# Two-kind attention and a four-expert MoE on one core: softmax sums by ones beside the values, exp(-ln) on ScalarE, an fp32 first group, and loads in another order

## The chip, the cores and the metric

The kernel runs on one core of a Trainium2 chip. A core has five engines, each with a queue of its own that it works through in order: TensorE (PE in the profile; its weight loads are PEld), VectorE (DVE), ScalarE (ACT), GpSimd (POOL) and SyncE (SP). DMAs are issued from SP, ACT and POOL; POOL's are the ones that can convert fp32 to fp16 on the way. The metric is the device time of one execution in microseconds, lower is better. Each time here is the median of three runs.

## The reference

Attention over 4 batches, 8 heads, 768 positions, head size 64, followed by a dense mixture of four experts. Heads 0, 2 and 6 are retrieval heads (plain causal); the five others are streaming heads, which see the first 4 positions and a window of 64.

```python
scores = scale * np.matmul(q, k.transpose(0, 1, 3, 2))
stream_keep = causal & (is_sink | in_win)          # n_sink = 4, window = 64
scores = np.where(mask, scores, -1e9); scores -= scores.max(-1, keepdims=True)
a = np.exp(scores); a = a / (a.sum(-1, keepdims=True) + 1e-9)
attn = np.matmul(a, v)                             # (4, 8, 768, 64)
x = attn.transpose(0, 2, 1, 3).reshape(3072, 512)
p = domain_probs / (domain_probs.sum(-1, keepdims=True) + 1e-9)
for e in range(4):
    out += p[:, e:e+1] * (np.maximum(x @ w1[e], 0) @ w2[e])   # 512 -> 1024 -> 512
```

The kernel takes exp without subtracting the maximum; the inputs are small.

## The kernel before

**Groups.** The 3072 rows are cut into eight groups of 384 rows, two per batch (`c` = 0 and 1). For each group there is an attention part, `attention(b, c)`, that leaves the transposed attention output `xT[g]` (512 x 384, fp16), and a MoE part, `moe_group(g)`, that needs it. The first half of a batch has scores against up to 384 keys, the second against up to 768 in retrieval heads.

**MoE.** Per expert, layer 1 is eight banks of four matmuls of 384 columns (L489), each bank evicted by a Relu on ScalarE (L496) into `hs`; layer 2 is three output tiles of eight matmuls of 512 columns (L502), each tile scaled by the row's probability and added into `acc` on VectorE (L514, L518). The weights of all experts stay in SBUF as fp16.

**Attention.** q and k arrive as fp16 and are transposed on PE against an identity (L302), two heads at a time (`transposes(hp)`); q goes to `qT` through ScalarE (L310), k to `kz` through VectorE (L317, L321, L326). `kz` is zero where the other head of the pair lies; in streaming heads it is kept in tiles of 96 keys with the 4 sink keys in front. `scores(h)` multiplies (L372), takes exp on ScalarE (L381) into `es` and multiplies by a 0/1 mask on VectorE (L385). `values(h)` multiplies `es` by v, with a column of ones as 65th column, so that row 64 of the PSUM bank holds the sums (L412). The sums go to `srow` (L425) and by a small DMA on SP into row h of `sums32` (L428); the values go to `av32` (L431). When all eight heads are through, three reciprocals (L461) and a cast (L463) make `rec16`, four matmuls with a selection matrix `sel` spread it over the partitions (L468), and four multiplies give `xT` (L475).

**Order.** Every engine's order is the order of the code. Attention of group 0 stands alone ahead of everything. After that the attention of group g + 1 is a generator whose steps are put between the steps of `moe_group(g)`, at a rate set by `begin`, `end` and `ATT`. All steps of the attention, the selection matmuls too, are thus spread over the MoE part before.

**Memory.** PSUM has eight banks: five for `pA` (transposes, scores, layer 1, the spread of the sums), one `pV`, two `pO`.

**Start.** k of group 0 comes as fp32 by SP and is cast on VectorE (L189), v as fp32 by ScalarE's and SP's queues and is cast between the heads (L196, L200, with the sink rows in L203), q by POOL with conversion (L178). POOL then builds the masks, loads w1 and w2 of expert 0, q, k and v of group 1, and the other weights, one DMA per head for q, k and v (L132, L133, L144). The kernel uses eight semaphores in turn for POOL's DMAs, so that the ninth waits until the first has landed.

Of the kernel before, what the change touches and what calls it, by code (L numbers as in the profile page):

```python
# [16 lines left out]
def kernel(  # L17
# [59 lines left out]
    )  # L77


    def bank():  # L80
        return pA.tile([P, 512], FP32, name="pA", bufs=5)
# [7 lines left out]
    vSf = []  # L89
    DV = D + 2  # L90
    for i in range(2):
        kz.append(
            [
                pers.tile([P, NT, P] if not RETR[h] else [P, S], FP16, name=f"kz{i}_{h}")
                for h in range(H)
            ]
        )
        vR.append(pers.tile([P, S // P, len(RH), DV], FP16, name=f"vR{i}"))
        vSf.append(pers.tile([P, NT * len(SH) * DV], FP16, name=f"vS{i}"))
        vS.append(vSf[i].rearrange("p (t s d) -> p t s d", t=NT, s=len(SH)))  # L100
# [12 lines left out]
    p_sb = pers.tile([P, NTILE, E], FP32, name="p_sb")  # L113

# [14 lines left out]
    def load_qk(b, c):  # L129
        alloc_qk(b, c)  # L130
        for h in range(H):
            nc.gpsimd.dma_start(out=q16[b, c][:, :, h, :], in_=rows_of(q, b, h, c))  # L132
            nc.gpsimd.dma_start(out=k16[b, c][:, :, h, :], in_=rows_of(k, b, h, c))  # L133
# [12 lines left out]
    def sink_rows(b):
        i = b % 2
        nc.vector.tensor_copy(
            out=vS[i][0:NS, :, :, 0:D],
            in_=vS[i][R0 : R0 + NS, 0:1, :, 0:D].to_broadcast([NS, NT, len(SH), D]),  # L150
        )

    def load_w1(e, f0, f1):
        nc.gpsimd.dma_start(
# [4 lines left out]
    def load_w2(e):  # L159
        nc.gpsimd.dma_start(  # L160
            out=w2sb[:, e * FTP : (e + 1) * FTP, :],
            in_=moe_w2[e].rearrange("(fo fi) d -> fi fo d", fi=P),
        )
# [4 lines left out]
    v32 = moe.tile([P, 4, H, D], FP32, name="v32", tag="hs", bufs=2)

    def load_v32(eng, h):  # L170
        if RETR[h]:
            eng.dma_start(out=v32[:, 0:3, h, :], in_=rows_of(v, 0, h, 0))
        else:
            eng.dma_start(out=v32[R0:P, :, h, :], in_=tiles_of(v, 0, h, 0))

    make_identity(nc, ident16)
    for h in range(H):
        nc.gpsimd.dma_start(out=q16[0, 0][:, :, h, :], in_=rows_of(q, 0, h, 0))  # L178
        nc.sync.dma_start(out=k32[:, :, h, :], in_=rows_of(k, 0, h, 0))
        if h < H // 2:  # L180
            load_v32(nc.scalar, h)
    for h in range(H // 2, H):
        load_v32(nc.sync, h)
    nc.sync.dma_start(
        out=probs, in_=moe_domain_probs.rearrange("(t p) e -> p t e", p=P)
    )

    def cast_k(hp):
        nc.vector.tensor_copy(  # L189
            out=k16[0, 0][:, :, 2 * hp : 2 * hp + 2, :],  # L190
            in_=k32[:, :, 2 * hp : 2 * hp + 2, :],
        )

    def cast_v(h):
        if RETR[h]:
            nc.vector.tensor_copy(out=v_dst(0, h, 0), in_=v32[:, 0:3, h, :])  # L196
            return
        s = SH.index(h)
        for r0, r1 in ((R0, 2 * R0), (2 * R0, P)):
            nc.vector.tensor_copy(  # L200
                out=vS[0][r0:r1, 0:TC, s, 0:D], in_=v32[r0:r1, :, h, :]
            )
        nc.vector.tensor_copy(  # L203
            out=vS[0][0:NS, :, s, 0:D],
            in_=vS[0][R0 : R0 + NS, 0:1, s, 0:D].to_broadcast([NS, NT, D]),
        )


    def zero(eng, t):
        if len(t.shape) == 3:  # L210
            t = t.rearrange("p a b -> p (a b)")
        eng.memset(t.bitcast(FP32), 0.0)

    def fixed_v(eng, i):
        eng.memset(vR[i][:, :, :, D : D + 1], 1.0)
        zero(eng, vSf[i][0:R0, :])
        eng.memset(vS[i][:, :, :, D : D + 1], 1.0)

    gp = nc.gpsimd
    gp.memset(mC, 1.0)  # L220
    for i in range(2):
# [378 lines left out]
```

## Time and profile before

| | |
|---|---|
| median of 3 runs (lowest, highest) | 510.93 us (509.07, 512.94) |
| profiled execution, and its span | 511.36 us, 509.5 us |
| PE busy / VectorE / ScalarE / POOL | 420.4 / 273.0 / 199.1 / 150.5 us |
| first matmul of layer 1, group 0 | at 64.83 us |
| first matmul of layer 1, group 1 | at 125.04 us |
| first matmul of layer 1, group 7 | at 463.65 us |
| mean granted PE clock | 0.982 |

Times inside the execution count from the first instruction. A row of the timeline gives the start, the length, the engine, the line, what is written and read, and how often; in brackets stand the idle time before it and what ended it. A row of the waits gives the total in us, how often, and the longest. A row of the groups gives the total busy time and the mean of one in ns. A row of a window gives its length, busy times, the granted clock, the share of the DMA engines and GB/s.

### The profile page before, as it was taken

The numbers are of one execution on the slowest core, as the hardware profiler recorded it, in microseconds if no ns is written. First come the engines' busy times: TensorE is split into PE (matmuls) and PEld (weight loads), VectorE is DVE, ScalarE is ACT, GpSimd is POOL, SyncE is SP. The second block draws the span as 40 slices with busy tenths as digits, with TensorE's granted clock in tenths as the row PEclk, the third lists the DMA queues.
The fourth block names the chain that finished last, engine by engine and source line by source line (L and its number), as shares of the span: only waits on it lengthen the run. The fifth ranks groups of instructions, "written<-read, shape, count | busy, mean of one in ns | idle before, by whom it ended". The sixth has DMA issues, their size and how long they took to land.

```text
span 509.5 us, 7014 instructions
## 1 busy us (share of the span) xinstructions
PE 420.4 (83%) x2616; PEld 238.7 (47%) x2616; DVE 273.0 (54%) x551; ACT 199.1 (39%) x441; POOL 150.5 (30%) x216
## 2 busy tenths in 40 slices
PE   0332199969997999969997999969978999969996
PEld 0221046634553555635553566535544556535553
DVE  1778535755775245665774245665774355562221
ACT  1121036632552355524542355524432354523332
POOL 8699137590094000950192000930000000000000
PEclk9999999998998999999998999999998999989999
DMA  9999999491086010861094010951000100001001
GB/s 158 184 70 164 210 164 58 25 68 59 7 56 39 1 62 2 52 43 63 1 66 28 22 43 1 60 35 63 2 1 1 50 13 2 0 2 62 1 0 62
DMA packets 92225, 25.50 MB, mean 50 GB/s; under 512 B 82464, under 2 KB 87584, under 8 KB 92192
## 3 DMA queue, kind: packets, MB, share of 16 engines
q0 software_dynamic: 77200, 17.05, 36.9%
q1 hardware_dynamic: 13392, 7.63, 5.4%
q10 hardware_dynamic: 1600, 0.39, 0.4%
q8 instruction: 20, 0.33, 0.3%
q14 instruction: 13, 0.11, 0.1%
HBM read 35.70 MB, written 6.29 MB: 82 GB/s over the span
## 4 chain that ended last, share of the span: by engine, by line
PE 72%; DVE 18%; DMA 3%; issue 2%; ACT 2%; POOL 2%; DVEq 0%; POOLq 0%
PE pA L489 30%; PE pO L502 29%; PE pV L412 5%; DVE rec L461 4%; PE pA L372 4%; DMA sums<-srow 3%; DVE srow L425 3%; PE pA L302 2%; DVE es L385 2%; DVE av L431 2%; PE pA L468 2%; DVE vS L200 1%; ACT es L381 1%; POOL q L178 1%; DVE kz L321 1%
## 5 line engine op out<-in xcount | busy, mean ns | idle before, releaser
L496 ACT ACTIVATE hs<-pA 128x384 f16<-128x384 f32 x256 | 126.0, 492 | 195.3 <-PE pA L489 187.2
L489 PE MATMUL pA<-xT,w1sb 128*128 128x384 f16 x1024 | 199.8, 335 | 0.0
L502 PE MATMUL pO<-w2sb,hs 128*128 128x512 f16 x768 | 181.6, 379 | 0.0
L489 PEld LDWEIGHTS <-w1sb 128*128 128x128 f16 x1024 | 99.4, 100 | 73.4 <-issue 19.9
L502 PEld LDWEIGHTS <-hs 128*128 128x128 f16 x768 | 73.3, 98 | 73.3
L518 DVE SCALAR_TENSOR_TENSOR acc<-pO,p_sb,acc 128x512 f32<-128x512 f32 x72 | 53.9, 749 | 96.5 <-PE pO L502 96.3
L381 ACT ACTIVATE es<-pA 128x256 f16<-128x256 f32 (+3 forms) x152 | 70.8, 479 | 75.1 <-PE pA L372 75.1
L132 POOL DMA_DIRECT2D q<-in_q_dram x56 | 43.3, 773 | 167.8 <-PE pA L302 158.8
L372 PE MATMUL pA<-qT,kz 128*128 128x160 f16 (+5 forms) x300 | 48.6, 255 | 0.0
L133 POOL DMA_DIRECT2D k<-in_k_dram x56 | 43.4, 776 | 16.1 <-DMA w2sb<-in_moe_w_dram 15.4
L385 DVE TENSOR_TENSOR es<-es,mS 128x320 f16<-128x320 f16 (+1 forms) x80 | 25.0, 315 | 42.0 <-ACT es L381 41.7
L425 DVE TENSOR_SCALAR srow<-pV 1x384 f32<-1x384 f32 x64 | 35.2, 551 | 14.5 <-PE pV L412 13.7
L412 PE MATMUL pV<-es,vS 128*65 128x160 f16 (+2 forms) x180 | 20.8, 234 | 26.2 <-DVE vS L203 16.1
L468 PE MATMUL pA<-rec,sel 128*128 128x384 f16 x32 | 12.1, 421 | 31.7 <-DVE rec L463 31.7
L431 DVE COPY av<-pV 64x384 f32<-64x384 f32 x64 | 35.3, 551 | 2.0
L372 PEld LDWEIGHTS <-kz 128*128 128x128 f16 x300 | 27.5, 103 | 18.4 <-issue 0.2
L412 PEld LDWEIGHTS <-vS 128*65 128x65 f16 x180 | 15.2, 117 | 33.7 <-DVE vS L203 18.0
L514 DVE TENSOR_SCALAR acc<-pO,p_sb 128x512 f32<-128x512 f32 x24 | 17.9, 746 | 21.6 <-PE pO L502 21.5
L412 PE MATMUL pV<-es,vR 128*65 128x384 f16 (+2 forms) x120 | 23.6, 289 | 6.5 <-DVE vR L196 4.3
L461 DVE RECIPROCAL rec<-sums 8x128 f32<-8x128 f32 x24 | 20.5, 902 | 11.7 <-DMA sums<-srow 10.9
L310 ACT ACTIVATE qT<-pA 128x384 f16<-128x384 f32 x32 | 15.7, 489 | 28.2 <-PE pA L302 28.2
L475 DVE TENSOR_TENSOR xT<-av,pA 128x384 f16<-128x384 f32 x32 | 17.1, 553 | 15.1 <-PE pA L468 15.1
(55 smaller groups left out, 196.5 us busy)
## 6 DMA issues: line engine op xcount, KB each, us to landing
out_dram<-acc SPq DMA_DIRECT2D x24, 256.0 KB, 2.0
w2sb<-in_moe_w_dram POOLq DMA_DIRECT2D x4, 1024.0 KB, 18.0
q<-in_q_dram POOLq DMA_DIRECT2D x64, 48.0 KB, 2.7
w1sb<-in_moe_w_dram POOLq DMA_DIRECT2D x3, 1024.0 KB, 17.9
k<-in_k_dram POOLq DMA_DIRECT2D x56, 48.0 KB, 2.6
vS<-in_v_dram POOLq DMA_DIRECT2D x35, 48.0 KB, 2.6
w1sb<-in_moe_w_dram POOLq DMA_DIRECT2D x2, 512.0 KB, 7.1
sums<-srow SPq DMA_DIRECT2D x64, 1.5 KB, 2.0
```

Source lines behind the costliest of these rows:

```text
L132: nc.gpsimd.dma_start(out=q16[b, c][:, :, h, :], in_=rows_of(q, b, h, c))
L133: nc.gpsimd.dma_start(out=k16[b, c][:, :, h, :], in_=rows_of(k, b, h, c))
L372: nc.tensor.matmul(out=ps[:, o : o + nq], lhsT=lhsT, rhs=qT[hp][:, q0 : q0 + nq], start=True, stop=True,)
L381: nc.scalar.activation(out=es[:, 0:cols], in_=ps[:, 0:cols], func=AF.Exp, scale=SC)
L412: nc.tensor.matmul(out=ps[:, q0 : q0 + nq], lhsT=lhsT, rhs=es[:, o : o + nq], start=(n == 0), stop=(n == len(work) - 1), skip_group_check= ...
L425: nc.vector.tensor_scalar(out=srow, in0=ps[D : D + 1, 0:CH], scalar1=1e-9, scalar2=None, op0=ALU.add)
L431: nc.vector.tensor_copy(out=av32[hp][u * D : (u + 1) * D, :], in_=ps[0:D, 0:CH])
L461: nc.vector.reciprocal(out=rec32[:, s], in_=sums32[:, s])
L489: nc.tensor.matmul(out=ps[:, 0:CH], lhsT=w1sb[:, e * DMP + ct, ft * P : (ft + 1) * P], rhs=xT[g][:, ct, :], start=(ct == 0), stop=(ct == D ...
L496: nc.scalar.activation(out=hs[:, ft, :], in_=ps[:, 0:CH], func=AF.Relu)
L502: nc.tensor.matmul(out=ps_o, lhsT=hs[:, ft, j * P : (j + 1) * P], rhs=w2sb[:, e * FTP + ft, :], start=(ft == 0), stop=(ft == FTP - 1),)
L518: nc.vector.scalar_tensor_tensor(out=acc[nt], in0=ps_o, scalar=p_ap, in1=acc[nt], op0=ALU.mult, op1=ALU.add,)
```

## The change

**Sums and division.** v of each head lies in 64 of 128 columns, and the other 64 are ones, so one values matmul leaves the values in one half of the partitions and the sum, repeated 64 times, in the other half. ScalarE takes `Ln` of the sums (with 1e-9 as bias) and `Exp` of the negative, in fp32, and one VectorE multiply per head writes `xT`. `srow`, `sums32`, `av32`, `rec32`, `rec16`, `sel` and the selection matmuls are gone. The multiply is put off until after the next head's first scores (`late`). One table set that holds both functions is loaded at the start. `qT` is now written by VectorE.

**PSUM.** `pA` has four banks, `pV` two; the first group uses `pO` for odd heads.

**First group.** q and k come as fp32 by SP and ScalarE and are transposed in fp32; the masks are added to the scores as -60000 by further matmuls against the identity; v is loaded by POOL with conversion. VectorE clears only the half of `kz` that group 0 needs. Eight matmuls on a zero tile stand ahead on PE. In groups after the first, the sink rows of v are copied by SP's DMAs, one per streaming head.

**Loads and pacing.** q and k of a half batch come as three DMAs each, of 128 rows with all heads. The order of the weights and of v changes, and batch 1's buffers are cleared after all weight loads. In expert 0 of group 0, the last of the four matmuls of a bank is put off until four banks have the other three. Attention steps are spread to 0.93 of the MoE part (2.6 experts in group 0, from 0.55 of an expert on).

```diff
@@ pools and tiles
-        return pA.tile([P, 512], FP32, name="pA", bufs=5)
+        return pA.tile([P, 512], FP32, name="pA", bufs=4)
-        vR.append(pers.tile([P, S // P, len(RH), DV], FP16, name=f"vR{i}"))
+        vR.append(pers.tile([P, S // P, len(RH), P], FP16, name=f"vR{i}"))
+        vS.append(pers.tile([P, NT, len(SH), P], FP16, name=f"vS{i}"))
@@ load_qk
+        for x, x16 in ((q, q16[b, c]), (k, k16[b, c])):
+            for j in range(3):
+                s0 = c * CH + j * P
+                gp.dma_start(
+                    out=x16[:, j, :, :],
+                    in_=x[b, :, s0 : s0 + P, :].rearrange("h p d -> p h d"),
+                )
@@ start
+        nc.sync.dma_start(out=k32[:, :, h, :], in_=rows_of(k, 0, h, 0))
+        eng = nc.scalar if h < 4 else nc.sync
+        eng.dma_start(out=q32[:, :, h, :], in_=rows_of(q, 0, h, 0))
...
+    one_values(nc.vector, 0, 0)
+    one_values(nc.scalar, 0, 1)
+    load_v(0, 0, [0, 1, 2, 3])
+    for h in range(H):
+        zero_keys(nc.vector, 0, h, 0)
...
+    mask_c(bC, 0.0, -60000.0)
+    mask_s(bS, 3, 0.0, -60000.0)
+    load_v(0, 0, [4, 5, 6, 7])
+    load_w1(0, 0, F)
     load_w2(0)
+    load_qk(0, 1)
+    load_w1(1, 0, F)
+    load_v(0, 1, range(H))
+    load_w2(1)
+    for e in range(2, E):
         load_w1(e, 0, F)
         load_w2(e)
@@ transposes
+                    if first:
+                        nc.tensor.transpose(o, i_, ident)
+                    else:
+                        nc.tensor.matmul(out=o, lhsT=i_, rhs=ident, start=True, stop=True)
-                    nc.scalar.activation(out=qT[hp], in_=ps[:, 0:CH], func=AF.Copy)
+                    nc.vector.tensor_copy(out=qT[hp], in_=ps[:, 0:CH])
@@ scores
+                if first:
+                    for m, mo, o0, o1 in masks:
+                        bias = bC if m is mC else bSf
+                        nc.tensor.matmul(
+                            out=ps[:, o0:o1], lhsT=ident16,
+                            rhs=bias[:, mo : mo + o1 - o0],
+                            start=False, stop=True, skip_group_check=True,
+                        )
...
+                run_late()
@@ values
-            nc.vector.tensor_scalar(
-                out=srow, in0=ps[D : D + 1, 0:CH], scalar1=1e-9, scalar2=None, op0=ALU.add
-            )
-            nc.sync.dma_start(out=sums32[h : h + 1, :], in_=srow)
+            nc.scalar.activation(
+                out=rc[r, :], in_=ps[o, 0:CH], func=AF.Ln, bias=eps[o, :]
+            )
+            def scale(r=r, ps=ps):
+                nc.vector.tensor_tensor(
+                    out=xT[g][r, hp, :], in0=ps[r, 0:CH], in1=rc[r, :], op=ALU.mult
+                )
+            if not pair:
+                nc.scalar.activation(out=rc[r, :], in_=rc[r, :], func=AF.Exp, scale=-1.0)
+                late.append(scale)
+            elif u == 0:
+                scale_of[hp] = scale
+            else:
+                nc.scalar.activation(out=rc, in_=rc, func=AF.Exp, scale=-1.0)
+                late.extend([scale_of[hp], scale])
@@ end of attention
-            nc.vector.reciprocal(out=rec32[:, s], in_=sums32[:, s])
...
-                lhsT=sel[:, hp * P : (hp + 1) * P],
-                rhs=rec16[g % 2],
+            for h in SH:
+                sink_rows(nc.sync.dma_start, b, h, c)
@@ moe_group
+            ahead = 4 if g == 0 and e == 0 else 1
@@ pacing
-        begin = UNIT if g == 0 else 0.0
-        end = 0.85 * E * UNIT
+        begin = 0.55 * UNIT if g == 0 else 0.0
+        end = 2.6 * UNIT if g == 0 else 0.93 * E * UNIT
+        att_ns = 6400.0 if pos == 0 else 10200.0
```

What stands where, at three places. First VectorE at the end of the attention for group 1, from the last head on. Before (L425 and L431 take head 7 out of `pV`, L518 belongs to the MoE, L317 is the next attention):

```order
L425 TENSOR_SCALAR srow<-pV 1x384
L431 COPY av_1021<-pV 64x384
L461 RECIPROCAL rec_1039<-sums_602 8x128 x3
L463 CAST rec_1_103<-rec_1039 8x384
L475 TENSOR_TENSOR xT<-av_724,pA 128x384
L475 TENSOR_TENSOR xT<-av_838,pA 128x384
L475 TENSOR_TENSOR xT<-av_915,pA 128x384
L475 TENSOR_TENSOR xT<-av_1021,pA 128x384
L518 SCALAR_TENSOR_TENSOR acc<-pO,p_sb,acc 128x512 x3
```

and now (L433 is the mask, L481 the multiply that writes `xT`, L588 the MoE's sum):

```order
L433 TENSOR_TENSOR es<-es,mC 128x128
L481 TENSOR_TENSOR xT<-pV,rc 64x384
L433 TENSOR_TENSOR es<-es,mS 128x384
L433 TENSOR_TENSOR es<-es,mS 128x256
L481 TENSOR_TENSOR xT<-pV,rc 64x384 x2
L588 SCALAR_TENSOR_TENSOR acc<-pO,p_sb,acc 128x512 x6
L337 CAST kz_0_87<-pA 64x384
```

Three sums of the MoE stood between the last write of `xT` and the next attention; now there are six, the sums of two experts.

Second ScalarE in the same attention, where streaming heads follow one another. Before (L381 is the exp of the scores, L496 the Relu):

```order
L381 ACTIVATE es<-pA 128x384
L496 ACTIVATE hs<-pA 128x384 x2
L381 ACTIVATE es<-pA 128x256
L496 ACTIVATE hs<-pA 128x384
L381 ACTIVATE es<-pA 128x384
L381 ACTIVATE es<-pA 128x256
```

and now (L429 is the exp of the scores, L476 the Ln, L486 the exp of its negative, `sk` the kept sink keys):

```order
L476 ACTIVATE rc<-pV,eps 64x384
L486 ACTIVATE rc<-rc 64x384
L358 COPY kz_7_84<-sk_313 64x4x4
L429 ACTIVATE es<-pA 128x384
L476 ACTIVATE rc<-pV,eps 64x384
L486 ACTIVATE rc<-rc 64x384
L429 ACTIVATE es<-pA 128x256
```

Two instructions per head have come between the exps.

Third POOL's queue near the start, from the last load for group 0 on. Before (L154 and L160 load w1 and w2, L132 and L133 q and k of group 1):

```order
L154 DMA w1sb<-in_moe_w_dram 128x4x512 x2
L160 DMA w2sb<-in_moe_w_dram 128x8x512
L261 MEMSET sel 128x512
L262 AFFINE_SELECT sel<-sel 128x512
L266 AFFINE_SELECT sel<-sel 128x512
L271 MEMSET rec_0_102 128x384
L271 MEMSET rec_1_103 128x384
L132 DMA q_177<-in_q_dram 128x3x64
L133 DMA k_178<-in_k_dram 128x3x64
```

and now (L154 and L158 load v, L171 and L177 the weights, L145 q and k):

```order
L158 DMA vS_86<-in_v_dram 96x4x64
L171 DMA w1sb<-in_moe_w_dram 128x4x1024
L177 DMA w2sb<-in_moe_w_dram 128x8x512
L145 DMA q_186<-in_q_dram 128x8x64 x3
L145 DMA k_187<-in_k_dram 128x8x64 x3
L171 DMA w1sb<-in_moe_w_dram 128x4x1024
L154 DMA vR_85<-in_v_dram 128x3x64
L158 DMA vS_86<-in_v_dram 96x4x64
```

Sixteen loads of q and k, one per head, have become six, and w1 of expert 1 stands ahead of v of group 1.

More of the change, by code (lines that the diff above doesn't have):

```diff
@@ L5 @@
 from concourse import bass_utils, mybir
+from concourse.act_sets import SETS
 from concourse._compat import with_exitstack
@@ L159, in load_w2 @@
     def load_w2(e):
-        nc.gpsimd.dma_start(
+        gp.dma_start(
             out=w2sb[:, e * FTP : (e + 1) * FTP, :],
@@ L163, in load_w2 @@
         )
-    alloc_qk(0, 0)
-    k32 = moe.tile([P, 3, H, D], FP32, name="k32", tag="hs", bufs=2)
[L168 to L176, printed above, removed]
+    ONES = 0.0078125 * (1.0 + 15360.0 * 2.0**-23)
+    ones = pers.tile([P, 1], FP32, name="ones")
@@ new lines, in one_values @@
+    def one_values(eng, i, c):
+        t = slice(3 * c, 3 * c + 3)
+        fill(eng, vR[i][:, t, :, D:P], ONES)
+        t = slice(TC * c, TC * (c + 1))
+        fill(eng, vS[i][0:R0, t, :, :].rearrange("p t h x -> p t (h x)"), ONES)
+        fill(eng, vS[i][:, t, 0:2, 0:D], ONES)
+        fill(eng, vS[i][:, t, 2, D:P], ONES)
+        fill(eng, vS[i][:, t, 3:5, 0:D], ONES)
+    assert all(h % 2 == 0 for h in RH) and [h % 2 for h in SH] == [1, 1, 0, 1, 1]
+    q32 = moe.tile([P, 3, H, D], FP32, name="q32", tag="hs", bufs=2)
@@ L209, in zero @@
[L209 to L221, printed above, removed]
+    nc.vector.memset(warm.bitcast(FP32), 0.0)
+    nc.vector.memset(eps, 1e-9)
+    nc.vector.memset(ones, ONES)
+    make_identity(nc, ident32)
@@ new lines, with warm_up, mask_c @@
+    one_values(nc.vector, 0, 0)
[3 more added lines that the diff above has]
+        zero_keys(nc.vector, 0, h, 0)
+    nc.vector.tensor_copy(out=ident16, in_=ident32)
+    ps_warm = pO.tile([P, DM], FP32, name="pO", bufs=2)
+    def warm_up(n, cols):
+        for _ in range(n):
+            nc.tensor.matmul(
+                out=ps_warm[:, 0:cols], lhsT=warm[:, 0:P], rhs=warm[:, 0:cols],
+                start=True, stop=True,
+            )
+    def mask_c(x, keep, drop):
+        gp.memset(x, keep)
+        for i in range(2):
+            gp.affine_select(
+                out=x[:, i * P : (i + 1) * P], in_=x[:, i * P : (i + 1) * P],
+                compare_op=ALU.is_ge, fill=drop, base=0, pattern=[[1, P]],
+                channel_multiplier=-1,
+            )
@@ L383, in scores @@
                 )
-                for m, mo, o0, o1 in masks:
+                for m, mo, o0, o1 in () if first else masks:
                     nc.vector.tensor_tensor(
@@ L395, in values @@
             hp, u = divmod(h, 2)
-            if first:
-                cast_v(h)
-            ps = pV.tile([D + 1, 512], FP32, name="pV", bufs=1)
+            if first and u == 1:
+                ps = pO.tile([P, 512], FP32, name="pO", bufs=2)
+            else:
+                ps = pV.tile([P, 512], FP32, name="pV", bufs=2)
             work = []
@@ L557 @@
             spent += ns
-            while done < (spent - begin) / (end - begin) * ATT:
+            while done < (spent - begin) / (end - begin) * att_ns:
                 step = next(att_steps, None)
```

331 lines of the change are left out of this document (167 added, 164 removed).

## The prediction

> **What bounds the kernel now.** I begin with the page: the span, the engines, the clock, and the chain that ended last.
>
> ```profile
> span 509.5 us, 7014 instructions
> PE 420.4 (83%) x2616; PEld 238.7 (47%) x2616; DVE 273.0 (54%) x551; ACT 199.1 (39%) x441; POOL 150.5 (30%) x216
> PE   0332199969997999969997999969978999969996
> PE 72%; DVE 18%; DMA 3%; issue 2%; ACT 2%; POOL 2%; DVEq 0%; POOLq 0%
> ```
>
> PE is the bound, with 89.1 us idle (509.5 − 420.4). The row of tenths puts that idleness in two places: the first five slices (64 us, mostly 0 to 3), and a dip that returns to the end. The list of waits names them.
>
> ```profile
> PE pA L468 <- DVE rec L463: 31.7, 8, 8.8
> PE pV L412 <- DVE vS L203: 16.1, 5, 5.7
> PE pA L302 <- DVE k L189: 13.3, 4, 9.4
> PE pV L412 <- DVE av L431: 6.9, 4, 1.9
> PE pV L412 <- DVE es L385: 4.6, 12, 0.7
> ```
>
> L468 waits eight times, once per group: 8.8 us in the first, 22.9 in the other seven, 3.3 each. L203, L189 and the 8.8 lie in the prologue, where nothing else can run. The end of attention for group 1 shows what such a wait is made of.
>
> ```profile
> 109.55 2.11 PE L489 MATMUL pA<-xT,w1sb 128*128 128x384 f16 x12
> 112.80 2.56 DVE L461 RECIPROCAL rec<-sums 8x128 f32<-8x128 f32 x3 [1.91 <-DMA sums<-srow]
> 115.87 0.82 PE L468 MATMUL pA<-rec,sel 128*128 128x384 f16 x2 [4.20 <-DVE rec L463]
> 116.00:118.00 2.00, 2.00 (x7) 0.50 0.00 0
> 125.04 0.81 PE L489 MATMUL pA<-xT,w1sb 128*128 128x384 f16 x4
> ```
>
> The last sums go through a DMA, three reciprocals and a cast; L468 stands in PE's queue waiting for them, and the MoE matmuls of the current group, which need none of this, stand behind L468. In the 2 us after the wait the granted clock is 0.50, so it costs more than its own length. 125.04 is the first matmul of group 1. Now the price of undisturbed work, and the six groups with attention between group 0 and the last.
>
> ```profile
> 165.18 5.34 PE L502 MATMUL pO<-w2sb,hs 128*128 128x512 f16 x24
> 170.36 5.36 PE L489 MATMUL pA<-xT,w1sb 128*128 128x384 f16 x32
> 175.56 4.70 PE L502 MATMUL pO<-w2sb,hs 128*128 128x512 f16 x21
> 125.04:463.65 338.61, 308.93 (x1963) 0.98 0.26 29
> 463.65 1.63 PE L489 MATMUL pA<-xT,w1sb 128*128 128x384 f16 x9
> ```
>
> From start to start layer 2 takes 5.18 us and layer 1 5.20, so one expert 10.38 and a group 41.5; one column costs 5.20 / (32 x 384) = 0.423 ns. Attention has 24 x 128 transpose columns and, in scores and values together, 10368 (first half of a batch) or 17920 (second half): 13440 and 20992 columns, 5.7 and 8.9 us. A pair of groups is therefore 2 x 41.5 + 14.6 = 97.6 us of undisturbed PE, against 338.6 / 3 = 112.9 measured. The 15.3 between: L468's waits 6.6, L412's about 3, the eight sel matmuls 8 x 384 x 0.423 ns = 1.3, the rest, some 4, the lower clock.
>
> **The change, part by part.** The sum has three pieces: group 0's end, three pairs, and the last group (463.65 to the end, 45.85), which stays.
>
> Normalisation. L425, L428, L431, L461, L463 and L468 go. Ln and Exp take their place on ScalarE, one multiply per head on VectorE, and no PE instruction: after the last values matmul PE's queue holds only MoE until the next group's first matmul wants xT. By the column count that last matmul now stands at 0.81 of the group, so 0.19 x 41.5 = 7.9 us of MoE cover Ln, Exp and multiply (about 0.5 + 0.5 + 0.55 from the rows below). If that cover were gone, the old wait would be back. With it L468's waits, its matmuls and the low clock leave a pair. VectorE sheds 64 x 2 instructions of 0.55 us and gains 32 more multiplies and 32 qT copies: it is no bound.
>
> ScalarE is what is late next. These are its prices.
>
> ```profile
> L496 ACT ACTIVATE hs<-pA 128x384 f16<-128x384 f32 x256 | 126.0, 492 | 195.3 <-PE pA L489 187.2
> L381 ACT ACTIVATE es<-pA 128x512 f16<-128x512 f32 x48 | 28.5, 596 | 11.8 <-PE pA L372 11.8
> L381 ACT ACTIVATE es<-pA 128x256 f16<-128x256 f32 x52 | 19.8, 381 | 48.6 <-PE pA L372 48.6
> L381 ACT ACTIVATE es<-pA 128x320 f16<-128x320 f32 x20 | 8.7, 434 | 5.4 <-PE pA L372 5.4
> L310 ACT ACT_TABLE_LOAD x1 | 1.3, 1283 | 3.0 <-issue 3.0
> ```
>
> The time follows the columns, so I take 0.49 us for a 64x384 Ln or Exp (bounds: 0.38, the 256-column row, and twice 0.49). 64 Ln and 61 Exp add 61 us, 32 qT copies leave with 16: 199 becomes some 245, still under 60% of the span. Ln joins Exp, Relu and Copy in one set of tables: ScalarE's instructions hold one table load as before, 1.28 us; were there two a head, it would be 164 us more. But a layer-1 phase is dense: eight Relu are 3.9 us in 5.2 us of PE plus some 1.4 of attention, 6.6. Where streaming heads fall into it (0.49 + 0.38 + 2 x 0.49 = 1.85 each for 0.56 us of PE), two heads and the start of the next bring 4.5, and 8.4 us of ScalarE stand against 6.6. Behind a late ScalarE instruction wait the next Relu and Exp, and PE for a free bank, of which pA now has four instead of five. One such phase falls in a second-half group, a milder one (7.0 against 6.1) twice in a first-half group. Layer 2 needs hs tile by tile and lets ScalarE catch up. Unabsorbed this is 5 us a pair, absorbed 0; I take 1.5, since three banks of 0.65 us nearly hold the 1.8. With the waits on the mask (L385, 4.6 / 3.5 pairs, say 1.2) a pair becomes 97.6 + 1.2 + 1.5 = **100.3**.
>
> The prologue. Before, it runs like this.
>
> ```profile
> 11.24 3.90 DVE L212 MEMSET kz<- 128x384 f32 x8
> 17.18 0.50 PE L302 MATMUL pA<-ident,k 128*128 128x128 f16 x3 [9.37 <-DVE k L189]
> 24.98 0.78 POOL L133 DMA_DIRECT2D k<-in_k_dram  x1 [3.88 <-DMA w2sb<-in_moe_w_dram]
> 43.60 4.26 DVE L200 CAST vS<-v 32x256 f16<-32x256 f32 x2
> 55.44 0.50 SPq L428 DMA_DIRECT2D sums<-srow  x1
> 64.83 6.82 PE L489 MATMUL pA<-xT,w1sb 128*128 128x384 f16 x32
> k<-in_k_dram SPq DMA_DIRECT2D x8, 96.0 KB, 4.3
> L321 DVE CAST kz<-pA 64x384 f16<-64x384 f32 x40 | 22.3, 557 | 1.1 <-PE pA L302 0.6
> L326 DVE CAST kz<-pA 64x32 f16<-64x32 f32 x20 | 3.7, 184 | 0.0
> L203 DVE COPY vS<-vS 4x512 f16<-4x512 f16 x5 | 2.1, 416 | 0.2
> ```
>
> VectorE waits for a mask and clears kz before it casts k, casts v between the heads (once 4.3 us), and 9.4 us pass from the last sum to the first MoE matmul. Afterwards q and k stay fp32 and are transposed as they land, v is cast by its DMA, the masks enter the scores on PE, and VectorE has only 3 us of clearing ahead. Pair 0's loads are issued by 1.9 and land by about 6 (4.3 us each); one set of transposes later, at 7, copies begin. From there VectorE owns 8 copies of 0.56, 10 small ones of 0.18, 4 qT and 8 multiplies of 0.55, 5 sink copies of 0.42: 15.0 us. ScalarE owns 3 x (0.60 + 0.38) + 5 x (0.43 + 0.38) + 13 x 0.49 = 13.4. Packed, that ends at 22. They feed one another through PE, so I add 4: MoE starts at **26** (22 to 34). An fp32 transpose is not in the trace: between the fp16 one (0.054 us) and four times that, 24 of them are 1.3 to 5.2 us of a PE that mostly waits here. The eight warm-up matmuls lie under the loads.
>
> Then group 0 runs while weights still come. Their pace:
>
> ```profile
> 25.00:42.40 17.40, 17.40 (x23) 1.00 1.11 84
> 42.40:73.00 30.60, 10.63 (x19) 1.00 1.23 199
> L132 POOL DMA_DIRECT2D q<-in_q_dram x56 | 43.3, 773 | 167.8 <-PE pA L302 158.8 <-DMA w1sb<-in_moe_w_dram 8.3 <-issue 0.5
> L154 POOL DMA_DIRECT2D w1sb<-in_moe_w_dram x5 | 3.8, 770 | 0.0
> L160 POOL DMA_DIRECT2D w2sb<-in_moe_w_dram x4 | 3.7, 914 | 0.0
> ```
>
> The columns are POOL's busy time, clock, DMA share and GB/s. w2 of expert 0 has landed at 24.98, where POOL goes on, and the queue ahead of it moves the same bytes after the change. Weights then come at some 200 GB/s, 5.2 us for a megabyte. Loads of q, k and v come slowly, and POOL is busy all the while: 48 KB per 0.77 us of issue is 64 GB/s. The change makes q and k of group 1 six loads of 1024 rows instead of sixteen of 384. At 0.91 each, the price of w2's issue with its 1024 rows, they are issued early and land 6 us after w2, at 31; if issue grows with rows, 2.06 each, they land at 37. PE meets their first transpose at 26 + 5.2 + 0.9 = 32. I take 31, since w1's 512 and w2's 1024 rows differ by 0.14 us only. w1 of expert 1 follows at 36 (wanted at 39), v by 41, w2 at 46 (wanted at 46), then one tensor per 5.2 us, no faster than PE uses them. I allow 1 us for waits here and 2 for ScalarE, since attention is squeezed into 0.15 to 0.58 of this group: 26 + 41.5 + 8.9 + 3 = **79.4** for its end, against 125.04. Two queues are reordered besides. POOL's clearing of batch 1's kz and values moves behind all weights and ahead of the loads for group 2; it fills a time in which eight transfers are under way and POOL can only wait. SP gets five sink copies per group in place of eight of sums; they wait for v, and behind them stand only outputs that come most of a group later.
>
> A rule speaks to this place: the Trainium skill, "DMA: Bandwidth & Descriptors", section "Anatomy of one DMA — SWDGE (gpsimd) path", says of descriptor generation that "You can emit a lot of descriptors before the incremental cost shows up". By it the six loads land at 31 and the sum stands as below; by a cost per row it is 7 us longer. The rows of 512 and 1024 agree with the rule; no run here shows 1024 rows that are cut this short.
>
> **Sum.** 79.4 + 3 x 100.3 + 45.85 = 426.2 us of span. The profiled execution took 511.36 us, 1.86 more than its span, and lies 0.4 above the median of 510.93. So 426.2 + 1.9 = **428 us**.
>
> **Rivals.**
> - ScalarE sets the pace: four banks don't absorb the dense phases, pairs cost 103.8, and group 0 gives 2 more: 428 + 10.5 + 2 = 441. For it: 8.4 against 6.6 us. Against it: ScalarE is idle 195 us ahead of the Relu alone.
> - The DMAs set the pace of group 0: q and k land at 37, each weight 6 us later, and PE stands still at 32 and again at expert 1, with the low clock behind it: 435. For it: small rows were never seen faster than 64 GB/s while only POOL loads ran. Against it: POOL was then the busy one.
> - The change doesn't do what it says: multiplies queue on VectorE behind accumulations that wait for PE, xT is late, and every group keeps its 3.3 us and the low clock behind: 3 x 10.5 + 4 more, 464. Against it: 7.9 us of cover.
> - Slower than before: without its pauses PE gets a lower clock. A dense stretch of the 20 us windows (columns: length, busy time of PE, of its weight loads, VectorE, ScalarE and POOL, then the clock):
>
> ```profile
> 180.00:200.00 20.00, 20.00 (x142) 12.24 (x140) 9.96 (x20) 12.41 (x28) 0.00 (x0) 1.00 0.08 28
> ```
>
> After its start PE has 332 + 53 = 385 us of full-clock matmuls. At a granted clock of 0.81 they are 90 us longer, 518. It decides from 0.82 on: 385 x (1 / 0.82 − 1) = 84.5, all that was won. For it: no stretch of this trace runs longer than some 60 us without a wait. Against it: PE is full in this window, and the clock is 1.00; the 0.98 of the six groups includes the low clock after each wait.
>
> The Trainium skill, "TensorE: Matmul & The Clock Gate", Part 1, knows a limit at 13/16 of the clock, but only "once three cores of a die run dense matmuls"; one core never trips it, and the dense stretches here agree.
>
> **How the numbers follow.** Forecast 0.64, ScalarE 0.15, DMAs 0.12, not hidden 0.05, clock 0.04. The forecast's own bounds run from 416 (start at 23, no stall on ScalarE, half the mask waits) to 438 (start at 34). The first two rivals together give 448; 415 to 450 leaves out the last two. Faster by over 1% is all but the clock, 0.95; within 1% (what a measurement of this kernel can just tell from no change) 0.01; slower 0.04.
>
> **What would show it.** No wait of PE between a group's last values matmul and the next group's first; the first MoE matmul near 26 and group 1's near 79; pairs near 100; one table load on ScalarE. The forecast is wrong if layer 1 shows idle PE before its banks, if the transposes of group 1 wait for k, if Ln takes much over 0.5 us, or if the clock falls in stretches without a pause.

## The result, and the profile after

The kernel after takes 428.39 us (median of 4 runs, 427.96 to 429.94), the kernel before 511.06 (median of 4 runs in the same series): a ratio of 0.8388, 95% interval 0.835 to 0.8427. The forecast was 428.0, in a range of 415 to 450. The profiled execution took 427.96 us, 1.96 more than its span.

The page of the kernel after: span, engines, the busy tenths of PE, and the shares of the chain that ended last.

```profile
span 426.0 us, 6784 instructions
PE 408.4 (96%) x2608; PEld 231.8 (54%) x2608; DVE 198.5 (47%) x433; ACT 251.7 (59%) x544; POOL 101.4 (24%) x155
PE   6689899999999999999999999999999999999996
PE 81%; ACT 8%; DMA 6%; POOL 2%; issue 2%; DVE 1%; POOLq 0%; ACTq 0%
```

PE's idle time has shrunk from 89.1 us to 17.6, and its row shows neither the empty prologue nor the dip that came back. PE's busy time fell by 12 us as well, though the warm-up matmuls, the fp32 transposes and the mask matmuls came in: the 32 selection matmuls are gone, and fewer matmuls ran at the low clock (the mean granted clock rose from 0.982 to 0.996). What each of the two brought is not separated. The list of waits for PE (total, how often, longest):

```profile
PE pV L457 <- DVE es L433: 1.8, 6, 0.6
PE pA L551 <- ACT hs L564: 1.7, 4, 0.6
PE pO L457 <- ACT es L429: 1.7, 2, 1.1
PE pA L326 <- DMA k<-in_k_dram: 1.6, 1, 1.6
PE pA L328 <- DMA k<-in_k_dram: 1.0, 3, 0.6
```

Nothing in it is longer than 1.6 us, where before there were waits of 9.4, 8.8 and 5.7. Where the division stood, a timeline across four engines now reads (the end of attention in a second-half group, and the first matmul of the next group):

```profile
219.88 0.27 PE L457 MATMUL pV<-es,vS 128*128 128x160 f16 x2 [0.28 <-DVE es L433]
219.99 2.76 PE L551 MATMUL pA<-xT,w1sb 128*128 128x384 f16 x16
220.19 0.57 ACT L476 ACTIVATE rc<-pV,eps 64x384 f32<-64x384 f32 x1 [0.20 <-PE pV L457]
220.80 0.52 ACT L486 ACTIVATE rc<-rc 64x384 f32<-64x384 f32 x1
221.35 0.56 DVE L481 TENSOR_TENSOR xT<-pV,rc 64x384 f16<-64x384 f32 x1 [1.06 <-ACT rc L486]
227.77 0.81 PE L551 MATMUL pA<-xT,w1sb 128*128 128x384 f16 x4
```

The chain Ln, Exp, multiply runs from 220.19 to 221.91 while PE goes on with the MoE of the current group; xT is ready 5.9 us before PE wants it. By windows (length, busy time of PE, clock, DMA share, GB/s), the stretches are:

```profile
21.45:31.13 9.68, 8.60 (x45) 0.84 1.87 180
31.13:79.56 48.43, 46.08 (x302) 1.00 1.39 169
79.56:380.32 300.76, 297.65 (x1939) 1.00 0.34 36
380.32:426.00 45.68, 41.68 (x225) 1.00 0.08 29
```

MoE starts at 21.45 (before at 64.83), group 1 at 79.56 (125.04), the last at 380.3 (463.65). Six groups take 300.76 us where they took 338.61, at a clock of 1.00. Of the 83.5 us that the span lost, 43.4 thus lie before the first MoE matmul, 2.1 in group 0 and 37.9 in the six groups.

### The profile page after: what moved, and what is told of

Read it like the earlier page. It is cut to its first block, busy times and chain, and to the rows that moved or that the text cites. A ratio compares the mean times of both kernels' runs of the same rounds, so it can differ in the third digit from the quotient of the medians.

```text
span 426.0 us, 6784 instructions
## 1 busy us (share of the span) xinstructions
PE 408.4 (96%) x2608; PEld 231.8 (54%) x2608; DVE 198.5 (47%) x433; ACT 251.7 (59%) x544; POOL 101.4 (24%) x155
## 4 chain that ended last, share of the span: by engine, by line
PE 81%; ACT 8%; DMA 6%; POOL 2%; issue 2%; DVE 1%; POOLq 0%; ACTq 0%
PE pO L572 38%; PE pA L551 32%; PE pV L457 5%; PE pA L411 4%; DMA w2sb<-in_moe_w_dram 3%; ACT hs L564 3%; DMA vR<-in_v_dram 2%; PE pA L328 2%; ACT rc L476 2%; ACT es L429 1%; ACT rc L486 1%; POOL vS L158 1%; POOL vR L154 1%; DVE kz L341 0%; DVE kz L337 0%
## 5 line engine op out<-in xcount | busy, mean ns | idle before, releaser
L429 ACT ACTIVATE es<-pA 128x256 f16<-128x256 f32 (+3 forms) x152 | 72.1, 486 | 47.0 <-PE pA L411 43.5
L588 DVE SCALAR_TENSOR_TENSOR acc<-pO,p_sb,acc 128x512 f32<-128x512 f32 x72 | 53.9, 749 | 76.9 <-PE pO L572 76.4
L145 POOL DMA_DIRECT2D q<-in_q_dram x21 | 18.6, 895 | 137.1 <-PE pA L411 81.3
L433 DVE TENSOR_TENSOR es<-es,mS 128x384 f16<-128x384 f16 (+1 forms) x70 | 22.2, 317 | 57.7 <-ACT es L429 56.9
L476 ACT ACTIVATE rc<-pV,eps 64x384 f32<-64x384 f32 x60 | 34.6, 576 | 24.2 <-PE pV L457 23.3
L481 DVE TENSOR_TENSOR xT<-pV,rc 64x384 f16<-64x384 f32 x60 | 33.2, 553 | 22.6 <-PE pA L551 11.2
L486 ACT ACTIVATE rc<-rc 64x384 f32<-64x384 f32 x58 | 30.2, 521 | 1.9
L158 POOL DMA_DIRECT2D vS<-in_v_dram x40 | 28.2, 710 | 9.9 <-DMA w2sb<-in_moe_w_dram 4.3
L433 DVE TENSOR_TENSOR es<-es,mC 128x256 f16<-128x256 f16 (+1 forms) x42 | 10.7, 256 | 36.9 <-ACT es L429 36.9
L584 DVE TENSOR_SCALAR acc<-pO,p_sb 128x512 f32<-128x512 f32 x24 | 18.0, 750 | 17.6 <-PE pO L572 17.5
L341 DVE CAST kz<-pA 64x384 f16<-64x384 f32 x40 | 22.3, 557 | 2.6 <-PE pA L328 1.1
L457 PE MATMUL pV<-es,vR 128*128 128x384 f16 (+2 forms) x120 | 21.7, 278 | 0.8 <-ACT es L429 0.7
L154 POOL DMA_DIRECT2D vR<-in_v_dram x24 | 18.5, 770 | 10.5 <-DMA w2sb<-in_moe_w_dram 5.4
L145 POOL DMA_DIRECT2D k<-in_k_dram x21 | 18.6, 910 | 4.5 <-DMA w2sb<-in_moe_w_dram 4.2
```

The lines of the kernel that those rows point to most:

```text
L145: gp.dma_start(out=x16[:, j, :, :], in_=x[b, :, s0 : s0 + P, :].rearrange("h p d -> p h d"),)
L429: nc.scalar.activation(out=es[:, 0:cols], in_=ps[:, 0:cols], func=AF.Exp, scale=SC)
L433: nc.vector.tensor_tensor(out=es[:, o0:o1], in0=es[:, o0:o1], in1=m[:, mo : mo + o1 - o0], op=ALU.mult,)
L457: nc.tensor.matmul(out=ps[:, q0 : q0 + nq], lhsT=v_tile(b, h)[:, t, :], rhs=es[:, o : o + nq], start=(n == 0), stop=(n == len(work) - 1), ...
L476: nc.scalar.activation(out=rc[r, :], in_=ps[o, 0:CH], func=AF.Ln, bias=eps[o, :])
L481: nc.vector.tensor_tensor(out=xT[g][r, hp, :], in0=ps[r, 0:CH], in1=rc[r, :], op=ALU.mult)
```

## The experiments

All of them are changes to the kernel after. In the timelines, line numbers are those of the kernel that ran. Of the changes to the first group's attention only the masks are taken back here; which of the others (the fp32 transposes, v converted by its DMA, the new division, the shorter clearing, the warm-up, the put-off matmuls) brings how much of the 43.4 us is read off the two traces and not shown by a run.

**The old division alone.** Groups 1 to 7 take back the one-row sums, their DMA, the reciprocals and the sel matmuls:

```
-  Ln, Exp on ScalarE and the multiply per head
+  srow <- ps row + 1e-9; DMA to sums32; 3 reciprocals, cast, 4 x matmul by sel, multiply
```

> Groups 1 to 7 take back the old division: the sum row is copied out, sent by a small DMA on SP, inverted in three reciprocals, and spread by four selection matmuls; group 0 and all else stay as in the changed kernel (srow, rec32 and av32 have fewer buffers than before the change, to fit). Theory A (what the six middle groups won is PE's wait for that division, its matmuls and the low clock behind it): a pair of groups goes from 100.2 us back to 110 to 113, group 0 gains 4 to 6, together 462 to 472 us, and PE waits some 3 us for the cast of the reciprocals once per group. Rival B (they were won by the second pV bank and a lighter VectorE): pairs stay under 104, the total under 442 us.

Measured 457.79 us, ratio 0.8935 (0.8897 to 0.8974). The selection matmul at the end of three attentions in a row, and the waits:

```profile
136.24 0.32 PE L575 MATMUL pA<-rec,sel 128*128 128x384 f16 x1 [0.99 <-DVE rec L571]
189.53 0.82 PE L575 MATMUL pA<-rec,sel 128*128 128x384 f16 x2 [2.86 <-DVE rec L571]
242.23 0.32 PE L575 MATMUL pA<-rec,sel 128*128 128x384 f16 x1 [0.96 <-DVE rec L571]
PE pA L575 <- DVE rec L571: 20.2, 7, 8.7
```

The wait is back, but at 3.8 us a pair, not 6.6, and the pair is 105.99 (136.24 to 242.23), 5.7 longer. Theory A has the mechanism and is too large; 7 of the 12.7 us that a pair won are still unaccounted for. (The wait of 8.7 us is in group 0, where 4 to 6 were expected.)

**The old pacing numbers on top of it.** From group 1 on:

```
+        if g > 0:
+            end = 0.85 * E * UNIT
+            att_ns = 10000.0
```

> The old division in groups 1 to 7 again (457.79 us, pair 105.99), now with the old pacing numbers as well from group 1 on: attention dealt out over 0.85 of the MoE part at 10000 ns, for both kinds of group. It tells where the other 6.9 us of the 12.7 us that a pair lost come from. Theory A, the pacing numbers: with one number for short and long attention the short groups leave early holes and the long ones crowd, stalls behind the division are as long as before the change (2.8 to 4.2 us, against 1.0 and 2.9), pair 108 to 111, time 465 to 472. Theory B, the pacing adds nothing: pair 105 to 107, 455 to 461.

Measured 489.03 us (0.9563, 0.9522 to 0.9604), more than either theory. The end of a second-half group in this kernel, first, and the clock behind it:

```profile
190.68 0.54 DVE L491 TENSOR_SCALAR srow<-pV 1x384 f32<-1x384 f32 x1
195.98 0.50 PE L575 MATMUL pA<-rec,sel 128*128 128x384 f16 x1 [4.18 <-DVE rec L571]
195.00:200.00 5.00, 4.02 (x13) 0.50 0.00 0
```

The same place in the kernel with the division alone:

```profile
184.24 0.54 DVE L491 TENSOR_SCALAR srow<-pV 1x384 f32<-1x384 f32 x1
190.00:195.00 5.00, 5.00 (x20) 0.76 0.02 5
```

From the last copy of sums to the sel matmul both need the same 5.3 us (190.68 to 195.98, and 184.24 to 189.53). What differs is how much MoE the pacing deals out meanwhile: the wait is 4.18 us against 2.86, and behind it the clock stays at 0.50 for 5 us against some 3. A pair is 114.8 us (mean of the two from 127.09 to 356.76): 8.8 us more from three numbers. PE's idle time makes 6.2 of them, 3.5 of it in the waits for the division; the list of waits has 8.1 us for masked scores (`es`) where the division alone has 2.6. The rest is busy time, with the low clock in it. So theory A, larger than expected: division and pacing together are the loss.

**One bank for the values product again, on top of both.**

```
-                ps = pV.tile([P, 512], FP32, name="pV", bufs=2)
+                ps = pV.tile([P, 512], FP32, name="pV", bufs=1)     # and pA bufs 4 -> 5
```

> As the run with the old division and the old pacing, and the values product has one bank again instead of two (the matmul banks five instead of four). Theory A, the single bank makes the next head's values matmul wait until both copies out of the bank are done (1.2 to 1.9 us for VectorE once a group before the change): pair 1.5 to 4 us above that run, and near the 112.9 of before. Theory B, the bank is free in time and the rest of the loss lies in the copies' smaller number of columns or in the SP queue: pair within 0.7 us of that run.

Measured 476.70 us (0.9314, 0.9277 to 0.9351): both theories fall, it is 12 us faster than the run before it. The end of a second-half group:

```profile
191.42 0.51 PE L473 MATMUL pV<-es,vS 128*128 128x64 f16 x5 [1.90 <-DVE rc L498]
191.76 4.39 PE L599 MATMUL pA<-xT,w1sb 128*128 128x384 f16 x16
197.27 0.34 PE L575 MATMUL pA<-rec,sel 128*128 128x384 f16 x1 [1.12 <-DVE rec L571]
190.00:195.00 5.00, 3.58 (x19) 0.77 0.01 1
195.00:200.00 5.00, 3.88 (x21) 0.89 0.01 2
```

The wait for the bank is there as expected, 1.90 us (L498 copies the values out of the bank), but ahead of the division, whose own wait sinks from 4.18 to 1.12: 3.0 us in two pieces in place of 4.2 in one. The low clock is not spared: it comes between the two waits, at 0.50 from 193 to 196, and the 16 matmuls at 191.76 take 4.39 us where they take 2.76 at full clock. PE's busy time per pair is that of the run before (104.0 and 104.1 us), so what was won is idle time, 7.9 us against 10.7. A pair is 111.9 (mean of 113.2 and 110.6), beside 112.9 before the change. The run also gave pA its fifth bank, so which of the two gained the 3 us is open; the two pairs of this run differ by nearly as much. The sum of the three steps, 5.7 + 8.8 − 2.9 = 11.6, accounts for the pair's 12.7 but for 1.1, in this order of steps. The old pacing with the new division was not run, so what the pacing costs by itself is open.

**Without cover behind the values.** Attention stretched over the whole MoE part, with the new division:

```
+        if g > 0:
+            end = E * UNIT
+            att_ns = 5500.0 if pos == 0 else 8700.0
```

> Only the pacing of groups 1 to 6 changes: the attention of the next group is stretched over the whole MoE part, so that its last values matmul stands at the group's end and no MoE matmuls of the old group are left behind it. Theory A (Ln, Exp and multiply cost nothing because 7.9 us of MoE cover them): each of six group ends shows a wait of PE of 1.3 to 2 us for xT, together 436 to 440 us, no low clock behind it. Rival B (the first three matmuls of each bank and the next group's work hide them anyway): under 430 us.

Measured 441.92 us (0.8635, 0.8582 to 0.8689). Two group starts:

```profile
129.75 0.32 PE L551 MATMUL pA<-xT,w1sb 128*128 128x384 f16 x1 [1.32 <-DVE xT L481]
184.00 0.32 PE L551 MATMUL pA<-xT,w1sb 128*128 128x384 f16 x1 [2.20 <-DVE xT L481]
184.00:188.00 4.00, 4.00 (x32) 1.00 0.03 6
```

Even the new chain is a wait when nothing covers it: theory A, a little dearer than expected, with 10.6 us of such waits at the six group ends out of the 13.5 that the run is longer. These waits left the clock at 1.00.

**Ln issued twice,** for more work on ScalarE:

```
+            nc.scalar.activation(out=rc[r, :], in_=ps[o, 0:CH], func=AF.Ln, bias=eps[o, :])
```

> Each Ln is issued twice, with the same result: ScalarE gets 64 x 0.58 = 37 us more, 289 us of some 430. Theory A (ScalarE has slack, its dense phases are caught up in layer 2): under 434 us. Rival B (ScalarE is close to being the bound, PE waits for a bank whenever it is late): half of the 37 us or more show, 445 us and above.

Measured 449.33 us (0.8777, 0.8741 to 0.8813): theory B. The page of this kernel has ScalarE busy for 286.8 us, 35.1 more than after and 64% of its span, and 21 of the 35 us show in the time. PE's waits for ScalarE add up to 21.1 us in its list, to 6.0 in the kernel after. A wait in a layer-1 phase, and the row that leads the list of waits:

```profile
170.53 0.81 PE L554 MATMUL pA<-xT,w1sb 128*128 128x384 f16 x4 [0.99 <-ACT hs L567]
PE pA L554 <- ACT hs L567: 8.8, 13, 1.7
```

**Two Relus of eight on VectorE,** the opposite:

```
+                    if ft in (3, 7):
+                        nc.vector.tensor_scalar(out=hs[:, ft, :], in0=ps[:, 0:CH],
+                                                scalar1=0.0, scalar2=None, op0=ALU.max)
```

> The Relus of tiles 3 and 7 of each expert go from ScalarE to VectorE (64 x 0.495 us, 31.7 us off ScalarE's 251.7). Theory A, ScalarE is close to the bound and its late Relus and exponentials cost TensorE small stalls (0.38 us for hs per pair, and some 2 us in group 0): 424.5 to 426.5. Theory B, those stalls are chance collisions, VectorE makes new ones (es masks queued behind Relus): 428 to 431.

Measured 426.79 us (0.8329, 0.8309 to 0.8348), 1.6 below the kernel after and between the theories. PE's wait for a Relu in each pair falls from 0.38 to 0.25 us, group 0 ends 0.2 us earlier, and w2 of expert 1 is now late there:

```profile
47.46 1.02 PE L578 MATMUL pO<-w2sb,hs 128*128 128x512 f16 x4 [0.51 <-DMA w2sb<-in_moe_w_dram]
229.24 0.82 PE L551 MATMUL pA<-xT,w1sb 128*128 128x384 f16 x4 [0.23 <-DVE kz L341]
```

The second row stands at 229.97 in the kernel after; from the one a pair before it (129.44 here, 129.72 there) the pair is 99.80, against 100.25.

**Sixteen q and k loads per group,** one for each head, as before the change:

```
-  6 x dma_start of 1024 rows (j = 0, 1, 2 of q and of k)
+  16 x dma_start of 384 rows (one head of q or of k)
```

> q and k of a group come again by sixteen DMAs of 384 rows, one per head, instead of six of 1024; nothing else changes. Theory A (POOL's issue time per DMA sets when these loads land, 0.77 us for 384 rows and 0.9 for 1024): k of group 1 lands at about 37 instead of 31, PE stands still near 30 for about 6 us, all weights come 6 us later, the clock falls once, and the total is 433 to 438 us. Rival B (the DMA engines take the same time per row, whoever issues them): within 1 us of the changed kernel, 427 to 430 us.

Measured 435.80 us (0.8511, 0.8476 to 0.8546). A's number, another place. PE in group 0, then POOL's issues in the same kernel:

```profile
41.52 0.82 PE L453 MATMUL pV<-es,vR 128*128 128x384 f16 x2 [6.68 <-DMA vR<-in_v_dram]
26.03 0.76 POOL L144 DMA_DIRECT2D k<-in_k_dram  x1 [4.08 <-DMA w2sb<-in_moe_w_dram]
33.62 0.74 POOL L150 DMA_DIRECT2D vR<-in_v_dram  x1
```

POOL issues each small load at 0.76 us. In both kernels it stands still until w2 has landed at 26; with ten more loads in front of it the first v goes out at 33.62, in the kernel after at 26.01. It is v that is late, not k.

**v ahead of w1 of expert 1.**

```
-    load_w1(1, 0, F)
     load_v(0, 1, range(H))
+    load_w1(1, 0, F)
```

> Only the order of two calls changes: the v loads of the second group are issued before w1 of the second expert, as attention would have it, and not behind it. Theory A, the order by time of use matters: w1(1) lands some 4 to 6 us later than its 36.0, TensorE waits for it or does attention work meanwhile; second group starts 2 to 5 us later than 79.56, time 430 to 434. Theory B, attention's steps in the same stretch are interchangeable with MoE's and the v that comes earlier gives back what w1 loses: within 1 us, 427.5 to 429.5.

Measured 430.71 us (0.8403, 0.8383 to 0.8422), 2.3 above the kernel after, theory A at its lower end; its row shows the wait:

```profile
40.61 0.82 PE L551 MATMUL pA<-xT,w1sb 128*128 128x384 f16 x4 [2.71 <-DMA w1sb<-in_moe_w_dram]
```

**Masks of group 0 back on VectorE.** The matmuls of bC and bS go, the multiplications of es come back:

```
-  matmul(ps[:, o0:o1], lhsT=ident16, rhs=bias) behind the scores of group 0
+  es *= 0/1 mask on VectorE, the masks made ahead
```

> Only the masks of group 0 go back to multiplications on VectorE behind each exponential (and the two 0/1 masks are made ahead of them); the fp32 transposes, the order of the loads and the sums by ones stay. The kernel after starts its first MoE matmul at 21.45 us. Theory A, VectorE was on the path of the first group and the masks on TensorE took it off: about 18 multiplications of 0.2 to 0.4 us stand between an exponential and its values matmul, some 5 us on VectorE, of which half shows: first MoE matmul at 24 to 25.5, time 430.5 to 433. Theory B, the first group is paced by its loads and by ScalarE: start within 1 us of 21.45, time 427.5 to 429.5.

Measured 428.31 us (0.8363, 0.8335 to 0.8392): theory B. MoE starts 0.5 us later, and PE then waits for k all the same:

```profile
21.95 0.84 PE L545 MATMUL pA<-xT,w1sb 128*128 128x384 f16 x2
30.74 0.23 PE L328 MATMUL pA<-ident,k 128*128 128x128 f16 x1 [0.64 <-DMA k<-in_k_dram]
```

Group 1 starts at 79.73, against 79.56: once k sets the pace at 31, a start half a microsecond earlier is worth next to nothing.

**Attention of group 1 spread over 3.7 units of group 0** instead of 2.6:

```
-        end = 2.6 * UNIT if g == 0 else 0.93 * E * UNIT
+        end = 3.7 * UNIT if g == 0 else 0.93 * E * UNIT
```

> In group 0 alone the attention of the next group is spread over 3.7 units of the MoE (instead of 2.6), so its exponentials, logarithms and Relus share ScalarE over a longer stretch and the masks and values come later. Theory A, group 0's excess over 44 us is ScalarE and VectorE being late in a dense stretch (waits of 0.5 to 0.64 us for hs and es at 40.9, 43.9 and 53.1 in the kernel after): 1.5 to 2.5 us shorter, 426 to 427. Theory B, the excess is the low clock and the k wait, which stay, or the spread's end brings an xT wait as at the pairs with no cover: 428 to 430.

Measured 430.56 us (0.8395, 0.837 to 0.8419): just above theory B's range, by a cause that neither named. The waits for masks at 53 to 56 are gone, as A had it, but:

```profile
47.50 1.87 PE L572 MATMUL pO<-w2sb,hs 128*128 128x512 f16 x4 [3.65 <-DMA w2sb<-in_moe_w_dram]
```

With less attention dealt out, PE reaches w2 of expert 1 before it lands, waits 3.65 us, and the first four matmuls behind the wait take 1.87 us, against 1.03 at full clock. The dense attention of group 0 was a cover for the weights.

**w2 of expert 1 ahead of the last two v loads,** with the two Relus on VectorE:

```
-    load_v(0, 1, range(H))
+    load_v(0, 1, range(6))
     load_w2(1)
+    load_v(0, 1, [6, 7])
```

> The Relus of tiles 3 and 7 on VectorE, as in the run that took 426.79, and w2 of the second expert is issued ahead of the v loads of heads 6 and 7, so that POOL's queue meets it before it has to wait for w1(1) to land (36.0). Theory A, group 0 is now bounded by its loads and w2(1) is the next one (0.51 us of wait at 47.46): w2(1) lands 1.5 to 2.5 us earlier, 425.5 to 426.6. Theory B, v of heads 6 and 7 is then late (it comes behind 1 MB of weights), 428 to 431.

Measured 427.14 us (0.8353, 0.8325 to 0.838). The wait for w2 has gone, but against 426.79 of the Relus alone nothing can be told apart.

**The same, spread over 3.1 units.**

> The same with the next group's attention in group 0 spread over 3.1 units instead of 2.6. Theory A, the spread to 3.7 lost (430.56) because it left TensorE without attention work while w2(1) was on its way (3.65 us of wait at 47.5), and with w2(1) earlier a moderate spread removes waits for masks at 53 to 56 (1.0 us) without that: 424.5 to 426. Theory B, what a spread loses ahead of w2(1) is more than it saves: 427 to 429.

Measured 425.79 us (0.8331, 0.8307 to 0.8354), the fastest kernel here: its runs, 425.40 to 427.02, lie below all of the kernel after, though the two intervals against before still touch. Group 1 starts and a pair ends at

```profile
78.67 0.81 PE L552 MATMUL pA<-xT,w1sb 128*128 128x384 f16 x4
228.53 0.82 PE L552 MATMUL pA<-xT,w1sb 128*128 128x384 f16 x4 [0.23 <-DVE kz L342]
```

0.9 and 1.4 us earlier than in the kernel after. That is theory A's number, but not its mechanism: PE still waits for masks, 2.1 us in all against 1.8 in the run before. In this execution the clock was 1.00 at 22 to 24, where it was 0.50 in the run before, and PE lost 1.8 us to a late Relu of VectorE instead. What makes it faster is open.

## Why the prediction was right, point by point

**The sum.** Group 0's end came at 79.56 (predicted 79.4), the pair at 100.25 (100.3), the last group at 45.7 (45.85). The first is right by luck, because two terms missed in opposite directions; the second is right in part by luck (see ScalarE). So 428 was met more closely than the working deserved.

**The start of MoE, 21.45 instead of 26.** It lies just below the range given for it, 22 to 34. That VectorE's 15 us packed behind 7 also end at 22 is chance. This is VectorE's last row for group 0:

```profile
23.57 0.56 DVE L481 TENSOR_TENSOR xT<-pO,rc 64x384 f16<-64x384 f32 x1 [0.60 <-ACT rc L486]
```

VectorE began its copies at 5.58 instead of 7 and was busy for 13.2 us instead of 15 up to 24.13; in between it stood idle for 5.4 us, most of it waiting for ScalarE, where 4 had been added for the engines feeding one another. What the sum left out is that MoE need not wait for the last multiply: with the last matmul of each bank put off, PE starts 2.7 us before that multiply ends. The fp32 transpose, bounded by 0.054 and 0.216 us, is about 0.11 (three start to start in 0.33 us), and the masks on PE bought 0.5 us of start (one execution of each kernel).

**Group 0, 58.1 us instead of 53.4.** The excess over the 50.4 us of matmuls is not the 3 us of the sum but 7.7. These rows of the kernel after carry most of it; the first is a window:

```profile
22.00:24.00 2.00, 2.00 (x7) 0.50 1.24 208
30.43 0.23 PE L328 MATMUL pA<-ident,k 128*128 128x128 f16 x1 [0.57 <-DMA k<-in_k_dram]
43.89 0.81 PE L551 MATMUL pA<-xT,w1sb 128*128 128x384 f16 x4 [0.58 <-ACT hs L564]
53.13 0.27 PE L457 MATMUL pV<-es,vS 128*128 128x160 f16 x2 [0.64 <-DVE es L433]
```

The first layer 1 runs partly at a clock of 0.50 and takes 7.0 us, not 5.2: a term that the sum left out. k lands at 31 as worked out, but PE, which starts 4.5 us sooner, waits 1.0 us for it; the prediction had named such a wait as a sign against it. Then come 2.35 us of idle time from 31.13 on, nearly all of it waits for ScalarE and VectorE, and some 2.5 us of busy time more than the columns ask for. So the 4.5 us won at the start were mostly lost again at k and in the low clock. In the execution with the spread over 3.7 units the clock at this place was 1.00, and PE only waited longer for k (1.9 us): a start this early could not be used.

**The loads.** The claim that a 1024-row load costs POOL little more than a 384-row load held. In the groups of the kernel after:

```profile
L145 POOL DMA_DIRECT2D q<-in_q_dram x21 | 18.6, 895 | 137.1 <-PE pA L411 81.3
L145 POOL DMA_DIRECT2D k<-in_k_dram x21 | 18.6, 910 | 4.5 <-DMA w2sb<-in_moe_w_dram 4.2
```

0.90 and 0.91 us each, against 0.77 for 384 rows; here the trace agrees with the rule of the Trainium skill that the prediction weighed. The rival of the DMAs was right about what stands closest behind: with per-head loads 435.80 was measured, its 435, but through v.

**The normalisation.** The old wait is gone from PE and 5.9 us of cover are left; taken away, 2.2 us of wait return. But the prediction made the division, the single bank and the low clock behind them responsible for the pair's loss. The runs split it: 5.7 us the division under the new pacing, 8.8 the old pacing with it, less about 3 that one bank gives back. That the pacing numbers decide how much MoE lies beside the division's 5.3 us was not in the prediction's account of the 15.3.

**ScalarE.** The term "Ln or Exp 0.49 us" was mis-sized:

```profile
L476 ACT ACTIVATE rc<-pV,eps 64x384 f32<-64x384 f32 x60 | 34.6, 576 | 24.2 <-PE pV L457 23.3
L486 ACT ACTIVATE rc<-rc 64x384 f32<-64x384 f32 x58 | 30.2, 521 | 1.9
L226 ACT ACT_TABLE_LOAD x1 | 1.3, 1283 | 2.9 <-issue 2.9
```

Ln took 0.576, Exp 0.521; 64 and 61 of them are 69 us where 61 were reckoned, and ScalarE is busy 251.7 instead of 245. The tables were loaded once, as said. Ln has its bias in a column of memory, as the Relus of 0.495 have not; the Trainium skill, "ScalarE: Activation LUTs", section "What ACT_TABLE_LOAD costs", puts such an operand at about 93 ns, and the trace shows 55 more than Exp. Exp reads `rc` and not a PSUM bank, and the Relus write fp16, so the operand's share is not isolated. The dense phases are absorbed: of the 1.5 us a pair that were set aside, 0.4 us of waits for hs came, the idle time of a pair is 1.0 in all, and the rest of what separates 100.25 from 97.6 is PE's busy time (99.2). So of the 2.7 us that the sum added for waits 1.0 came, and 1.6 us of busy time that the column count lacks made up the number. As the clock is 1.00 here, the 4 us a pair that the prediction put down to the low clock before were too many by about as much (an estimate from these two busy times). The rival in which ScalarE sets the pace was not far: 35 us more of Ln cost 21.

**The clock.** The rival on the other side is refuted in one row above: 300.76 us nearly without a pause at 1.00.

## What to carry to other kernels

A chain across three engines that ends a stage is not to be shortened alone: what counts is how much independent work the order of PE's queue leaves beside it, and a pacing number can be worth more than the chain (8.8 against 5.7 us a pair here, with the old division in place). Look at what a removed wait was covering: when work left its place in group 0, the next load was what PE met (k at 31 with the earlier start, w2 at 47 with fewer late Relus or less attention). And an engine at 59% can be nearly the bound where its work comes in phases; adding a doubled instruction tells it in one run.

## What the runs showed of the hardware

- The length of a wait of PE does not by itself tell the clock behind it (read in windows of 1 us). Behind waits of 0.96 to 1.32, 2.20, 2.71, 2.76 and 2.80 us it stayed at 1.00. Behind 2.82 and 2.86 (the old division alone) it was 0.50 for some 3 us. Behind six waits of 3.12 to 3.16 (the two runs with the old pacing) it stayed at 1.00 twice and fell to 0.50 four times, once only a microsecond later. Behind 3.55, 3.65, 4.18, 4.20 and 6.68 it was 0.50 for 3 to 5 us, behind 4.16 too, a microsecond late. But behind 1.90 it fell to 0.50 in the run with one bank and stayed at 1.00 in the kernel before. And it came where PE was merely thin: at 0.50 at 22 to 24 in the kernel after, with no wait over 1.13 us ahead of it since 7, and in two other kernels at the same stretch (the spreads over 3.7 and 3.1 units) not at all. The Trainium skill, "TensorE: Matmul & The Clock Gate", Part 1, speaks of a free-running window of about 3.4 us, which would fit that equal waits end differently; an idle window of that length, taken as one without any matmul, does not fit the falls behind 1.90 and 2.82 us, and there the measurement decides. No run here shows the window itself.
- An instruction of DMA issue on POOL costs 0.67 to 0.92 us in the kernel after, from 48 KB to 1 MB; the number of loads, more than their size, filled POOL's queue.
